# Conditioning scale and shift applied in one step ahead of the first projections, in an adaLN transformer block on one Trainium2 core

## The chip, the core and the metric

The kernel runs on one core of a Trainium2 chip. The metric is device time in microseconds (us) for one execution. Its engines are PE (TensorE, matrix products), DVE (VectorE), ACT (ScalarE), POOL (GpSimd) and SP (SyncE, which here only issues DMAs). Each engine works through its own list in order; semaphores tie the lists together.

## The reference, cut to what matters

```python
# x: (1, 2048, 512) bf16; 32 heads of 16; every query sees 8 keys, 2 rows apart, backwards
mod = (silu(c) @ w_mod).reshape(1, 6, 1, 512)
sa, ca, ga, sb, cb, gb = mod[:, 0..5]            # shift, scale, gate; twice
h = layernorm(x) * (1 + ca) + sa
x = x + ga * A(h, wqkv, wo)      # A: q, k, v = h @ wqkv; softmax over 8 keys; @ wo
h = layernorm(x) * (1 + cb) + sb
x = x + gb * B(h, w1, w3, w2)    # B: (silu(h @ w1) * (h @ w3)) @ w2, F = 1792
```

## The kernel before, in words

The 2048 rows are 16 tiles T of 128 rows. `_build` records some 1200 operations, each with its engine, the values that it reads and writes, and a function that emits it. No run-time scheduler exists: the constant `ORDER` fixes one sequence of all operations, which is split into the five engines' lists, and `SLOTS` gives each temporary value its buffer (8 PSUM banks, and pools of SBUF tiles). `Program.synchronize` then adds only the waits that are needed. Each engine is strictly in order, so one instruction that waits holds up all that stands behind it on that engine. All DMAs but the one for `c` are issued by SP, in order too.

The stages, which overlap:

- **Conditioning.** `c` goes through a tanh (L468), two small POOL operations (L470, L471), a PE transpose (L473) and an ACT copy to `csz` (L475). `scales` (L481) multiplies the scale columns of `w_mod`, by 128-row pieces (512 columns, 1 KB rows, L490), and leaves 1 + ca in `modc`. `warm` (L543) puts in matmuls of ones, whose results are not used. `shifts` (L503) comes later: it forms sa from its own load of 512 KB, and `kb`, the product of sa and wk (32 one-column matmuls, L509).
- **First norm.** `ln_stats` does mean and variance of a tile on DVE (L598, L599), the inverse root on POOL (L603, L605), and the normalised tile `xn` on DVE (L610); tile 3's sums are on ACT (`moments`, L581, L584).
- **First four tiles.** `first_keys` (L700) turns `xn` on PE (L716), scales it without the shift into `h` (L726, L727), multiplies it with wk at 256 columns for tiles 0 and 1 (L735), then for tiles 2 and 3 (L745), adds `kb` on the way out of PSUM (L755), and adds sa to `h` afterwards on DVE (L763) for q and v.
- **Projections.** The other tiles go in groups of four: PE turns (L672), ACT scale and shift (L680), 16 q and 16 k matmuls of 512 columns (L781), and 4 v matmuls a tile (L800). v goes to DRAM and comes back shifted (`values`).
- **Attention.** For each tile DVE makes the products q·k for 8 offsets (L832), PE sums them over each head (L843), DVE and ACT do the softmax for two tiles at a time (L858 to L891), PE turns the weights (L901), DVE multiplies them into the shifted v (L928), PE sums (L936). The sums are turned on PE and copied by ACT for tiles in `EARLY` (0 to 3; L949, L953), whose shifted v comes in 4 KB packets; for the others an SP DMA turns them, and v comes in 2 KB packets. Then wo (L962) and the residual (L966).
- **Feed-forward.** Second norm, w1 and w3 matmuls (L978), silu and product, w2 (L1021, L1009), residual (L1037), store. These are interleaved with the attention of later tiles.

Of the kernel before, what the change touches and what calls it, by code (L numbers as in the profile page):

```python
# [7 lines left out]
ALU = mybir.AluOpType  # L8
AX = mybir.AxisListType

P = 128
# [257 lines left out]
EARLY = frozenset((0, 1, 2, 3))  # L269
PACKET = {T: 170 if T in EARLY else 88 for T in range(16)}  # L270
WMOD = 66
WKP = 88
WARMS = (8, 1, 1, 1, 3)
NVB = 6
NOB = 4
DMA_T = (3, 2)
KEV = (0, 1, 2, 3)
STACT = (3,)
UPACT = frozenset((g, f) for g in range(4) for f in range(14))
GBLATE = False  # L280
LN1 = [[0, 1, 2, 3], [4, 5, 6, 7], [8, 9, 10, 11], [12, 13, 14, 15]]


def _build(p, A_x, A_wqkv, A_wo, B_w1, B_w3, B_w2, c, w_mod, out):
# [46 lines left out]
    sab = sb([P, KT], bf, "sab")  # L331
    kb = sb([P, KT], f32, "kb")
# [93 lines left out]
    for T in range(4):  # L426
        p.dma(x_sb[:, T, :], x_view[:, T, :], ("load", 1), (128, 1024), w=[vx[T]])
    vwm0 = [Val(f"wms0_{t}") for t in range(KT)]
    for t in range(KT):
        p.dma(wm_s[0][:, t, D:2 * D], wm_view[:, t, D:2 * D], ("load", 2), (128, 1024), w=[vwm0[t]], again=WMOD)  # L430
    vwq = [Val("wq"), [Val("wk0"), Val("wk1")], Val("wv")]
    vwq[1] = [vwq[1][t % 2] for t in range(KT)]
    wqkv_view = A_wqkv.rearrange("(t p) n -> p t n", p=P)
    for i in range(2):
        p.dma(wqkv[:, i::2, D:2 * D], wqkv_view[:, i::2, D:2 * D], ("load", 4), (256, 1024), w=[vwq[1][i]], again=WKP)
    vwsa = Val("wms0_sa")
    p.dma(wm_s[0][:, :, 0:D], wm_view[:, :, 0:D], ("load", 28), (512, 1024), w=[vwsa])
    for i in (0, 2):
        p.dma(wqkv[:, :, i * D:(i + 1) * D], wqkv_view[:, :, i * D:(i + 1) * D], ("load", 3 + i), (512, 1024), w=[vwq[i]])
    for g in range(1, 4):  # L440
        p.dma(x_sb[:, 4 * g:4 * g + 4, :], x_view[:, 4 * g:4 * g + 4, :], ("load", 5 + g), (512, 1024), w=vx[4 * g:4 * g + 4])
# [20 lines left out]
    for g in range(NG):  # L462
# [7 lines left out]
    p.op("pool", lambda e: e.tensor_scalar(thc[:], thc[:], 1.0, None, op0=ALU.add), 250, k, w=[vthc])  # L470
    p.op("pool", lambda e: e.tensor_tensor(c4s[:], thc[:], c4[:], ALU.mult), 300, k, r=[vthc, vcT], w=[vc4])  # L471
# [3 lines left out]
    p.op("act", lambda e: e.activation(csz[:, :, 7], bank(vpc).bitcast(bf)[:, 0:KT], ACT.Copy, scale=0.5), 180, ("mod", 1),  # L475
         r=[vpc, vcsz], w=[vcs])

    vca, vsa, vsab, vkb, vmodB = Val("ca"), Val("sa"), Val("sab"), Val("kb"), Val("modB")
    vg = [Val("ga"), Val("gb")]

    def scales():  # L481
        k = ("mod", 2)
        vm = Val("ps_mod", psum)

        def mm(e, t):
            b = bank(vm)
            if t == 0:
                e.matmul(b[:, 0:KT], ident[:], mbase[:, 4:8], start=True, stop=False)
            for j in range(KT):
                ins = e.matmul(b[:, 0:KT], wm_s[0][:, t, D + j * P:D + (j + 1) * P], csz[:, t, 7 - j:11 - j], start=False,  # L490
                               stop=(t == KT - 1 and j == KT - 1))
            return ins

        o = None
        for t in range(KT):
            after = warm(WARMS[t])
            o = p.op("pe", lambda e, t=t: mm(e, t), (4 + (t == 0)) * 27, k, r=[vwm0[t], vcs, vident, vbase] + wm_hold, part=[vm],
                     after=after + ([o] if o else []))
            last[0] = o
        p.op("dve", lambda e: e.tensor_copy(modc[:, 4:8], bank(vm)[:, 0:KT]), 100, k, r=[vm], w=[vca])  # L500

    def shifts():
        k = ("mod", 11)  # L503
        vm, vb = Val("ps_mod", psum), Val("ps_kb", psum)

        def columns(e, v, lhs, rhs):
            for j in range(KT):
                for t in range(KT):
                    ins = e.matmul(bank(v)[:, j:j + 1], lhs[:, t, j * P:(j + 1) * P], rhs(t), start=(t == 0), stop=(t == KT - 1))  # L509
            return ins  # L510

        p.op("pe", lambda e: columns(e, vm, wm_s[0], lambda t: csz[:, t, 7:8]), 16 * 27, k, r=[vwsa, vcs] + wm_hold, w=[vm])
        p.op("dve", lambda e: e.tensor_copy(sab[:], bank(vm)[:, 0:KT]), 100, k, r=[vm], w=[vsab])
        p.op("dve", lambda e: e.tensor_copy(modc[:, 0:4], bank(vm)[:, 0:KT]), 100, k, r=[vm], w=[vsa])
        p.op("pe", lambda e: columns(e, vb, wqkv[:, :, D:2 * D], lambda t: sab[:, t:t + 1]), 16 * 27, ("mod", 12),
             r=[vsab] + vwq[1] + qkv_hold, w=[vb])
        p.op("dve", lambda e: e.tensor_copy(kb[:], bank(vb)[:, 0:KT]), 100, ("mod", 12), r=[vb], w=[vkb])

    def modulation():
        k = ("mod", 3)  # L520
        vm = Val("ps_mod", psum)

        def mm(e):
            b = bank(vm)
            e.matmul(b[:, 0:8], ident[:], mbase[:], start=True, stop=False)
            for t in range(KT):
                for j in range(8):
                    ins = e.matmul(b[:, 0:8], wm_s[1][:, t, j * P:(j + 1) * P], csz[:, t, 7 - j:15 - j], start=False,
                                   stop=(t == KT - 1 and j == 7))
            return ins  # L530

        p.op("pe", mm, 33 * 27, k, r=[vwms[1], vcs, vident, vbase] + wm_hold, w=[vm])
        p.op("dve", lambda e: e.tensor_copy(modc[:, 8:16], bank(vm)[:, 0:8]), 100, k, r=[vm], w=[vmodB])
# [43 lines left out]
    def moments(T):  # L577

        k = ("st", T)
        vs, vb, vm, vv, vn = Val("sum"), Val("nmean"), Val("mean"), Val("var"), Val("xn", xnpool)  # L580
        p.op("act", lambda e: e.activation(vn.at[:], x_sb[:, T, :], ACT.Identity, accum_out=sx[:, T, :]), c_act(512) + 212, k,  # L581
             r=[vx[T]], w=[vs, vn])
        p.op("dve", lambda e: e.tensor_scalar(nm[:, T, :], sx[:, T, :], -D ** -1.5, None, op0=ALU.mult), C_TINY, k, r=[vs], w=[vb])
        p.op("act", lambda e: e.activation(vn.at[:], x_sb[:, T, :], ACT.Square, bias=nm[:, T, :], scale=D ** -0.5,  # L584
                                           accum_out=mv[:, T, 1:2]), c_act(512) + 212, k, r=[vx[T], vb], w=[vv, vn])
        p.op("dve", lambda e: e.tensor_scalar(mv[:, T, 0:1], sx[:, T, :], 1.0 / D, None, op0=ALU.mult), C_TINY, k, r=[vs], w=[vm])
        return [vv, vm]

    def ln_stats(Ts):
# [3 lines left out]
        for T in Ts:  # L593
            vs, vm = Val("st"), Val("mv")
            if T in STACT:
                vms += moments(T)
                continue
# [5 lines left out]
        o = p.op("pool" if i > 1 else "dve", lambda e: e.tensor_scalar(rsn, mv[:, i:i + n, 1], EPS, None, op0=ALU.add), 250 if i > 1 else C_TINY, k,  # L603
                 r=vms, w=[va])
        p.op("pool", lambda e: e.tensor_tensor(rsn, rsn, bass.AP(cst, 0, [[1, P], [0, n]]), ALU.pow), 600, k, r=[va, vcst],  # L605
             w=[vr], lead=o if i > 1 else None)
# [36 lines left out]
    def ln_T(which, gi, vns):  # L643
        vh = Val("h", hpool)
        vh.pieces = None
        k0 = 2 * (gi + 1) if not which else 2 * gi + 2 * len(LN1) + 2
        modv = [vmodB] if which else [vca, vsa]
        n = len(vns)
        if gi >= DMA_T[which]:
            k = ("tr", k0)  # L650
# [530 lines left out]
```

## Time and profile before

| what | value |
|---|---|
| median of the runs | 242.81 us (242.54 to 243.16, 3 runs) |
| the profiled execution: its own time | 241.96 us |
| its span in the profile | 239.9 us |
| PE busy | 232.0 us (97%) |
| DVE busy | 169.0 us (70%) |
| ACT busy | 159.9 us (67%) |
| POOL busy | 20.6 us (9%) |
| DMA moved | 39.92 MB, mean 166 GB/s |

The profile is of one execution. About 2.1 us of its own time lie outside its span. A busy time counts an instruction from start to end; PE's matmuls overlap, so for PE the distance from one start to the next (the pitch) is used where work is added up.

### The profile page before, as it was taken

How to read it: one execution, taken by the hardware profiler on the slowest of the kernel's cores; microseconds unless marked ns; L12 is line 12 of the kernel's file. 1: busy time of each engine (PE TensorE's matmuls, PEld its weight loads, DVE VectorE, ACT ScalarE, POOL GpSimd, SP SyncE). 2: the span in 40 equal slices, each digit the busy share in tenths (PEclk: the TensorE clock that was granted, in tenths of full speed). 3: DMA queues.
4: the chain of work that ended last, by engine and by line, in shares of the span. 5: the costliest groups of instructions: out<-in, count | busy, mean ns of one | idle time of the engine just before them, and what ended most of it. 6: DMA issues, size and time to landing. Idle time of an engine off the chain costs nothing.

```text
span 239.9 us, 4608 instructions
## 1 busy us (share of the span) xinstructions
PE 232.0 (97%) x1803; PEld 135.6 (57%) x1831; DVE 169.0 (70%) x295; ACT 159.9 (67%) x328; POOL 20.6 (9%) x53
## 2 busy tenths in 40 slices
PE   7899999999999999999999999999999999999995
PEld 2655546444578766764444444444654446686774
DVE  5588999999999999989999687282531412334342
ACT  4349786799999987698768898775745385231310
POOL 5524020002001000110000110010000010000000
PEclk9999999999999999999999999999999999999999
DMA  6999788599899698799751864613310001200011
GB/s 172 286 359 300 229 268 256 110 344 378 281 305 321 216 247 212 209 286 192 210 147 36 261 223 117 174 67 68 104 49 0 4 0 44 68 0 22 3 45 44
DMA packets 43418, 39.92 MB, mean 166 GB/s; under 512 B 17249, under 2 KB 35717, under 8 KB 43397
## 3 DMA queue, kind: packets, MB, share of 16 engines
q1 hardware_dynamic: 43389, 39.63, 56.5%
q8 instruction: 14, 0.23, 0.4%
q14 instruction: 7, 0.06, 0.1%
q10 hardware_dynamic: 8, 0.00, 0.0%
HBM read 29.62 MB, written 6.33 MB: 150 GB/s over the span
## 4 chain that ended last, share of the span: by engine, by line
PE 87%; DMA 4%; SPq 3%; DVE 2%; ACT 1%; issue 1%
PE pall L978 41%; PE pall L1021 18%; PE pall L781 8%; PE pall L962 5%; DMA sb_x<-in_A_x_dram 4%; PE pall L800 4%; PE pall L936 3%; PE pall L843 3%; SPq L124 3%; PE pall L1009 3%; DVE sb_st L598 1%; PE pall L672 1%; PE pall L901 1%; DVE sb_xn L610 0%; ACT sb_hh L988 0%
## 5 line engine op out<-in xcount | busy, mean ns | idle before, releaser
L978 PE MATMUL pall<-sb_h,sb_w 128*128 128x256 bf16 (+1 forms) x666 | 102.4, 308 | 0.4 <-issue 0.2
L978 PEld LDWEIGHTS pall<-sb_h,sb_w 128*128 128x128 bf16 x672 | 64.9, 98 | 36.2 <-ACT sb_sg L984 0.9
L984 ACT ACTIVATE sb_sg<-pall 128x256 bf16<-128x256 f32 (+1 forms) x84 | 35.6, 458 | 27.5 <-PE pall L978 27.1
L1021 PE MATMUL pall<-sb_w,sb_hh 128*128 128x512 bf16 x189 | 44.6, 379 | 0.5 <-issue 0.2
L988 ACT ACTIVATE sb_hh<-pall 128x256 bf16<-128x256 f32 (+1 forms) x56 | 26.5, 499 | 17.6 <-PE pall L978 17.3
L832 DVE TENSOR_TENSOR sb_pq<-sb_q,sb_kT 128x4096 bf16<-128x4096 bf16 x16 | 36.1, 2279 | 0.0
L928 DVE TENSOR_TENSOR sb_vsh<-sb_vsh,sb_al 128x4096 bf16<-128x4096 bf16 x14 | 31.9, 2286 | 0.2 <-ACT sb_al L905 0.2
L1021 PEld LDWEIGHTS pall<-sb_w,sb_hh 128*128 128x128 bf16 x196 | 19.0, 98 | 20.9 <-issue 0.4
L781 PE MATMUL pall<-sb_h,sb_wqkv 128*128 128x512 bf16 x106 | 26.0, 379 | 0.4 <-issue 0.2
L989 DVE TENSOR_TENSOR sb_hh<-sb_sg,sb_hh 128x256 bf16<-128x256 bf16 (+1 forms) x56 | 17.8, 352 | 9.0 <-ACT sb_hh L988 8.9
L1037 DVE TENSOR_TENSOR sb_o<-pall,sb_x 128x512 bf16<-128x512 f32 (+1 forms) x18 | 11.2, 628 | 16.6 <-PE pall L1021 12.9
L992 DVE TENSOR_TENSOR sb_hh<-sb_sg,pall 128x256 bf16<-128x256 bf16 x28 | 10.8, 418 | 15.8 <-PE pall L978 11.6
L966 DVE SCALAR_TENSOR_TENSOR sb_x<-pall,sb_x 128x512 bf16<-128x512 f32 x16 | 10.8, 686 | 11.5 <-PE pall L962 11.5
L781 PEld LDWEIGHTS pall<-sb_h,sb_wqkv 128*128 128x128 bf16 x112 | 10.2, 98 | 11.9 <-issue 1.1
L630 POOL TENSOR_SCALAR sb_rs<-sb_var 128x2 f32<-128x2 f32 x8 | 2.5, 314 | 155.5 <-ACT sb_xn L624 155.5
L962 PE MATMUL pall<-sb_wo,sb_ot 128*128 128x512 bf16 x61 | 15.4, 379 | 0.3 <-issue 0.2
L800 PE MATMUL pall<-sb_wqkv,sb_h 128*128 128x512 bf16 x58 | 14.8, 379 | 0.4 <-issue 0.2
L657 ACT ACTIVATE sb_h<-sb_h,sb_modc 128x512 bf16<-128x512 bf16 (+1 forms) x20 | 13.5, 727 | 0.9 <-DMA sb_h<-sb_xn 0.9
L635 ACT ACTIVATE sb_xn<-sb_x,sb_nb,sb_rs 128x512 bf16<-128x512 bf16 x16 | 12.5, 818 | 1.9 <-DVE sb_nb L632 1.9
L942 ACT ACTIVATE sb_oa<-pall 128x512 bf16<-128x512 f32 x16 | 9.3, 604 | 4.7 <-PE pall L936 4.7
L624 ACT ACTIVATE sb_xn<-sb_x,sb_nm 128x512 bf16<-128x512 bf16 x16 | 11.6, 725 | 1.1 <-DVE sb_nm L620 1.0
L789 ACT ACTIVATE sb_q<-pall 128x512 bf16<-128x512 f32 x16 | 9.5, 607 | 3.6 <-PE pall L781 3.6
(114 smaller groups left out, 235.8 us busy)
## 6 DMA issues: line engine op xcount, KB each, us to landing
sb_vsh<-v_scratch_dram SPq DMA_DIRECT2D x40, 256.0 KB, 3.5
v_scratch_dram<-sb_v SPq DMA_DIRECT2D x16, 256.0 KB, 4.7
sb_vsh<-v_scratch_dram SPq DMA_DIRECT2D x8, 512.0 KB, 6.4
sb_w<-in_B_w_dram SPq DMA_DIRECT2D x6, 512.0 KB, 8.9
sb_w<-in_B_w_dram SPq DMA_DIRECT2D x6, 384.0 KB, 6.5
sb_vshx<-v_scratch_dram SPq DMA_DIRECT2D x8, 256.0 KB, 4.1
out_dram<-sb_o SPq DMA_DIRECT2D x14, 128.0 KB, 1.8
sb_x<-in_A_x_dram SPq DMA_DIRECT2D x3, 512.0 KB, 10.1
```

Source lines behind the costliest of these rows:

```text
L635: p.op("act", lambda e, vn=vn, T=T: e.activation(vn.at[:], x_sb[:, T, :], ACT.Identity, bias=nb[:, T, :], scale=rs[:, NT + T, :]), c_act(5 ...
L657: return e.activation(vh.at[:, ft, 0:n * P], vh.at[:, ft, 0:n * P], ACT.Identity, bias=modc[:, 8 * which + ft:8 * which + ft + 1], scale=m ...
L781: ins = e.matmul(bank(vp)[:, 0:n], wqkv[:, t, kind * D + ft * P:kind * D + (ft + 1) * P], vh.at[:, t, 0:n], start=(t == ORDER[0]), stop=(t ...
L800: ins = e.matmul(bank(vp), vh.at[:, t, tt * P:(tt + 1) * P], wqkv[:, t, 2 * D:3 * D], start=(t == ORDER[0]), stop=(t == ORDER[-1]))
L832: return e.tensor_tensor(vp.at[:], in0, in1, ALU.mult)
L928: return e.tensor_tensor(v_w, v_w, a_w, ALU.mult)
L962: ins = e.matmul(bank(vy), vt.at[:, ft, :], wo[:, ft, :], start=(ft == 0), stop=(ft == KT - 1))
L978: ins = e.matmul(bank(vp)[:, 0:n], wt[:, t, fi * P:(fi + 1) * P], vh.at[:, t, 0:n], start=(t == 0), stop=(t == KT - 1))
L984: p.op("act", lambda e: e.activation(vt.at[:, 0:n], bank(vgp)[:, 0:n], ACT.Silu), c_act(n), k, r=[vgp], w=[vt], table="silu")
L988: p.op("act", lambda e: e.activation(vh_.at[:, 0:n], bank(vup)[:, 0:n], ACT.Copy), c_act(n), k, r=[vup], w=[vh_])
L989: p.op("dve", lambda e: e.tensor_tensor(vh_.at[:, 0:n], vt.at[:, 0:n], vh_.at[:, 0:n], ALU.mult), 60 + n * 69 // 128, k, r=[vt], w=[vh_], ...
L1021: ins = e.matmul(bank(vz), vhh[fi].at[:, tt * P:(tt + 1) * P], w2[:, fi, :], start=(fi == 0), stop=(fi == NF - 1))
```

## The change

Scale and shift of the first norm are formed together, before anything is projected. `scales` and `shifts` go; `modulation(0)` multiplies both halves (8 columns at once) from rows of 2 KB, in four loads of 256 KB, as `modulation(1)` does for the second norm. `first_keys`, `moments`, `kb` and the late addition of sa go. Tiles 0 and 1, and tiles 2 and 3, become two groups of `ln_T`, whose ACT and DVE evictions apply scale and shift; q and k are both multiplied at 256 columns for these groups, and for the first group each matmul waits only for its own piece of `h` and its half of wk or wq. The loads come in a new order (tiles 0 and 1, w_mod, wk in halves, tiles 2 and 3, wq in halves, wv, and so on). Tiles 2 and 3 leave `EARLY`, so their sums are turned by DMA, and their shifted v comes in 2 KB packets. The small conditioning steps move from POOL and ACT to DVE, `ln_stats` adds epsilon on POOL for tiles 0 and 1 too, `warm` is called 21 times and not 14, and `ORDER` and `SLOTS` are new throughout.

```diff
-EARLY = frozenset((0, 1, 2, 3))
+EARLY = frozenset((0, 1))
-WARMS = (8, 1, 1, 1, 3)
+WARMS = (8, 3, 2, 2, 6)
+DEV = 2
-DMA_T = (3, 2)
-KEV = (0, 1, 2, 3)
-STACT = (3,)
+DMA_T = (4, 2)
-LN1 = [[0, 1, 2, 3], [4, 5, 6, 7], [8, 9, 10, 11], [12, 13, 14, 15]]
+LN1 = [[0, 1], [2, 3], [4, 5, 6, 7], [8, 9, 10, 11], [12, 13, 14, 15]]
...
-    for T in range(4):
+    for T in range(2):
         p.dma(x_sb[:, T, :], x_view[:, T, :], ("load", 1), (128, 1024), w=[vx[T]])
     for t in range(KT):
-        p.dma(wm_s[0][:, t, D:2 * D], wm_view[:, t, D:2 * D], ("load", 2), (128, 1024), w=[vwm0[t]], again=WMOD)
+        p.dma(wm_s[0][:, t, :], wm_view[:, t, 0:1024], ("load", 2), (128, 2048), w=[vwm0[t]], again=WMOD)
+    p.dma(x_sb[:, 2:4, :], x_view[:, 2:4, :], ("load", 27), (256, 1024), w=vx[2:4])
...
-    p.dma(wm_s[0][:, :, 0:D], wm_view[:, :, 0:D], ("load", 28), (512, 1024), w=[vwsa])
+    for i in range(2):
+        p.dma(wqkv[:, i::2, 0:D], wqkv_view[:, i::2, 0:D], ("load", 3), (256, 1024), w=[vwq[0][i]])
+    p.dma(wqkv[:, :, 2 * D:3 * D], wqkv_view[:, :, 2 * D:3 * D], ("load", 5), (512, 1024), w=[vwq[2][0]])
+    for T in (4, 6):
+        p.dma(x_sb[:, T:T + 2, :], x_view[:, T:T + 2, :], ("load", 6), (256, 1024), w=vx[T:T + 2])
...
-    p.op("pool", lambda e: e.tensor_scalar(thc[:], thc[:], 1.0, None, op0=ALU.add), 250, k, w=[vthc])
-    p.op("pool", lambda e: e.tensor_tensor(c4s[:], thc[:], c4[:], ALU.mult), 300, k, r=[vthc, vcT], w=[vc4])
+    p.op("dve", lambda e: e.scalar_tensor_tensor(c4s[:], thc[:], 1.0, c4[:], op0=ALU.add, op1=ALU.mult), 180, k,
+         r=[vthc, vcT], w=[vc4])
+    p.op("dve", lambda e: e.tensor_scalar(c4s[:], c4s[:], 0.5, None, op0=ALU.mult), 180, k, w=[vc4])
...
+        for ts in ([(t,) for t in range(KT)] if i == 0 else [tuple(range(KT))]):
+            after = warm(WARMS[ts[0]]) if i == 0 else []
+            o = p.op("pe", lambda e, ts=ts: mm(e, ts), (8 * len(ts) + (ts[0] == 0)) * 27, k,
+                     r=[vwms[1]] * i + [vwm0[t] for t in ts] * (1 - i) + [vcs, vident, vbase] + wm_hold, part=[vm],
+                     after=after + ([o] if o else []))
+        p.op("dve", lambda e: e.tensor_copy(modc[:, jlo:jlo + 8], bank(vm)[:, 0:8]), 100, k, r=[vm], w=[vmod[i]])
...
+        vh.pieces = [Val(f"h_{ft}") for ft in range(KT)] if not which and not gi else None
...
+                def ev_dve(e, j=j, vt=vt, half=half):
+                    ft = 2 * half + j
+                    b = bank(vt).bitcast(bf)
+                    return e.tensor_scalar(vh.at[:, ft, 0:n * P], b[:, j * 512:j * 512 + n * P],
+                                           modc[:, 8 * which + 4 + ft:8 * which + 5 + ft],
+                                           modc[:, 8 * which + ft:8 * which + ft + 1], op0=ALU.mult, op1=ALU.add)
...
-            o = p.op("pe", lambda e, t=t: mm(e, (t,)), c_mm(n), k, r=[vh.pieces[t]] + vw + qkv_hold, part=[vp], hold=[vh],
+            o = p.op("pe", lambda e, t=t: mm(e, (t,)), c_mm(n), k, r=[vh.pieces[t], vw[t]] + qkv_hold, part=[vp], hold=[vh],
...
-    scales()
+    modulation(0)
     warm(WARMS[4])
-    shifts()
     for gi, Ts in enumerate(LN1):
-        if gi == 0:
-            vh = first_keys([[v for T in (0, 1) for v in ln_stats([T])], ln_stats([2, 3])])
-        else:
-            vh = ln_T(0, gi, [v for pr in pairs(Ts) for v in ln_stats(pr)])
+        vns = [v for pr in ([[T] for T in Ts] if gi == 0 else pairs(Ts)) for v in ln_stats(pr)]
+        vh = ln_T(0, gi, vns)
         proj_qk(gi, Ts, 0, vh)
-        if gi:
-            proj_qk(gi, Ts, 1, vh)
+        proj_qk(gi, Ts, 1, vh)
```

## The prediction

> **What bounds the kernel now.** First the page: PE's share, then where in the span it is idle.
>
> ```profile
> span 239.9 us, 4608 instructions
> PE 232.0 (97%) x1803; PEld 135.6 (57%) x1831; DVE 169.0 (70%) x295; ACT 159.9 (67%) x328; POOL 20.6 (9%) x53
> ...
> PE   7899999999999999999999999999999999999995
> PEld 2655546444578766764444444444654446686774
> DVE  5588999999999999989999687282531412334342
> ```
>
> PE is full from the third slice to the last but one. DVE is full with it up to slice 21 (126 us). The windows, with each engine's busy time:
>
> ```profile
> 0.00:8.40 8.40, 6.39 (x40) 2.51 (x40) 5.27 (x18) 4.16 (x9) 4.77 (x20) 1.00 0.68 203
> 8.40:14.00 5.60, 4.84 (x70) 4.16 (x72) 2.59 (x12) 0.92 (x3) 2.00 (x6) 1.00 0.99 317
> ...
> 40.00:60.00 20.00, 19.73 (x179) 9.76 (x180) 19.74 (x21) 18.49 (x36) 1.35 (x2) 1.00 0.85 269
> 60.00:80.00 20.00, 19.84 (x197) 14.38 (x199) 19.62 (x26) 19.79 (x49) 1.02 (x2) 1.00 0.93 304
> ```
>
> Columns: stretch, length, then PE, PEld, DVE, ACT, POOL; granted clock, DMA share, GB/s. So any order that lets DVE start its attention work later must either have DVE catch up or make PE wait. The timeline gives the few real PE gaps, DVE's first product and a late meeting of both:
>
> ```profile
> 8.46 1.03 PE L735 MATMUL pall<-sb_h,sb_wqkv 128*128 128x256 bf16 x8 [0.45 <-DVE sb_xn L610]
> 11.43 0.54 PE L509 MATMUL pall<-sb_csz,sb_wm_s 128*128 128x1 bf16 x16 [0.62 <-DMA sb_wm_s<-in_w_mod_dram]
> 22.47 0.29 PE L672 MATMUL pall<-sb_ident,sb_xn 128*128 128x128 bf16 x2 [0.44 <-DVE sb_xn L610]
> 24.77 4.46 DVE L832 TENSOR_TENSOR sb_pq<-sb_q,sb_kT 128x4096 bf16<-128x4096 bf16 x2
> 112.66 2.28 DVE L928 TENSOR_TENSOR sb_vsh<-sb_vsh,sb_al 128x4096 bf16<-128x4096 bf16 x1
> 115.07 1.04 PE L936 MATMUL pall<-sb_vsh,sb_ind 128*32 128x512 bf16 x16
> ```
>
> By distances between matmul starts the gaps are 0.6 us before 8.46, 0.8 before 11.43 and 0.6 before 22.47; after that none above 0.3 us but for matmuls missing from the records. The first gap really ends with wk's first half, which landed at 8.33. Nothing behind 22.5 us can be won by better order; the change can win only in the front or by less PE work, and any wait that it adds costs in full.
>
> **PE work.** Pitches from the trace: 0.216 us for 512 columns, 0.109 for 256, 0.058 for a 128-column turn, 0.026 for a 1- to 8-column matmul. Gone: 32 shift matmuls (0.83), 8 turns of tiles 2 and 3 (0.46). Scale and shift together are 33 small matmuls for 17 (+0.42); q of the first four tiles is 32 x 0.109 for 16 x 0.216 (+0.03). Sum about -0.9. The seven added warm-up matmuls lie ahead of the first projection, where PE waits for loads anyway.
>
> **Loads of the front.** The trace's landing records give, for the queue of before: 0.5 MiB at 4.67 us, 1.0 at 6.63, 1.25 at 8.33, 1.5 at 9.54, 2.0 at 11.30, 2.5 at 12.85, 3.0 at 14.34, 3.5 at 15.85, 4.0 at 18.70. In the new queue the end of w_mod stands at 1.25 MiB, wk's halves at 1.5 and 1.75, tiles 2 and 3 at 2.0, wq's halves at 2.25 and 2.5, wv at 3.0, tiles 4/5 at 3.25, 6/7 at 3.5, 8 to 11 at 4.0. Longer rows bring nothing by themselves: in the packet records 1 KB took 51 ns and 2 KB (the later w_mod load, the shifted v) 101 to 103. Bigger loads do help: SP needs 0.46 us to issue each, and at 128 KB each the DMA engines were idle for 14% of 2.2 to 6.7 and 6% of 6.7 to 9.6, together 0.8 us.
>
> ```profile
> 2.20:6.70 4.50, 4.39 (x28) 1.59 (x27) 3.49 (x12) 2.48 (x7) 2.26 (x5) 1.00 0.86 245
> 6.70:9.60 2.90, 2.45 (x28) 1.71 (x25) 1.99 (x6) 0.84 (x2) 2.46 (x7) 1.00 0.94 305
> ...
> 12.90:16.00 3.10, 3.02 (x31) 1.76 (x31) 2.43 (x10) 0.79 (x2) 0.04 (x1) 1.00 1.10 367
> ```
>
> Landings are thus the old ones at equal bytes, less 0 to 0.8; I take 0.4, as part of that idle will be landing skew.
>
> **The new front, walked.** w_mod ends at 7.9. Eight matmuls (0.2), the copy to `modc` (0.16), two evictions each on DVE (0.3 each) and ACT (0.4 each), and six warm-ups: first k matmul at about 9.4, 0.9 later than now. PE then follows the loads: wk's halves, wq's first (11.7), wq's second (12.45), and 11 matmuls after it: 13.65. Tiles 2 and 3 land at 10.9; two statistics (0.64 each), aggregates (0.2), POOL's pair (0.26 + 0.71), two normalisations (0.4 each) and hand-overs put their turns at 14.3 to 14.8. Tile 3's statistics now cost DVE 0.7, but the four additions of sa (1.2) are gone. From 14.8 PE has v, 24 q/k matmuls and v again (5.2 us): 20.0. Then turns, both gates, 8 q/k and 4 v matmuls (4.4 us), with a stall on the normalised tile 7: DVE has evictions until 15.6, four statistics to 18.2, two normalisations to 19.2, the statistics of 8 and 9 (landed 18.3) to 20.5, tile 7 at 21.3, where PE would be at 20.9: 0.5. So the projections of tiles 4 to 7 begin at 24.9 (24.5 to 25.4). Lateness (start of a row less the pitches ahead of it, so all idleness and half-speed so far) is 24.9 - 19.4 = 5.5 there, against 5.9 before at 29.27. All pitches sum to 230.4 (with the warm-ups, +1.5) against 229.9. By PE alone: 5.5 + 230.4 - 5.9 - 229.9 = +0.1 us. ACT does not decide: its 256-column evictions follow at 0.27 us, its 512-column ones at 0.48, and it loses two turned-sum copies (0.74 each) and tile 3's sums (1.7 us).
>
> **DVE behind it.** Before the first product DVE still has statistics of 10 to 13, four normalisations, four aggregates and the two gate copies. The same from 20.05 to 24.77 before took 4.7 us with one statistic more and a copy less: 4.4. First product at 25.7 (25.3 to 26.2), against 24.77. From there to the end of tile 9's weighting DVE has the same list in both kernels: 14 products, 10 weightings, 28 feed-forward products, 8 residuals, five softmax ends, the wo scaling and four of w2. It took 114.86 - 24.77 = 90.1 us, so tile 9 is ready at 115.9. PE's sum of it began at about 115.55 (half of the row above is tile 8's), with 120.6 us of pitches behind; now 121.1 lie behind, as the new order keeps more for later. So +0.35 + 0.5 = +0.85 us. This is the later path, and the forecast: span 239.9 + 0.9 = 240.8, that execution 242.8; on the median 242.81 + 0.9 = 243.7. Since DVE sat idle about 1.9 us within those 90 us, the term can fall to the +0.1 above (below, if the loads are early); with 26.2 and another 0.5 us of waits it is +1.9.
>
> **Tiles 2 and 3 by DMA.** SP gets two more turns (1.25 us each to issue, landing in 2.4 to 5.1) and four more loads of v. PE's turn and ACT's copy go; PE has 4 us of other rows before it needs the result, so I cost them at nothing. Without that cover each is 2 to 4 us late. Behind the two turns SP holds a v store and the loads of v for tiles 4 and 5; they wait for ACT's copies at about 66, would issue from 68.5, and land by 74.4 and 77.5, against use from 77.3 and 80. The margin is about 3 us.
>
> **Small moves.** POOL's two conditioning steps (0.53 and 0.42) become two on DVE and the copy to `csz` moves from ACT to DVE (0.15 to 0.2 each, by L603 and L475). They push tile 1's statistics back by about 0.6, and epsilon for tiles 0 and 1 goes from DVE (0.15) to POOL (0.2 to 0.4 each). Both normalised tiles are then ready by about 7.0, under w_mod's end at 7.9; were w_mod landed at 6.5, they would cost 0.5. On SP the zero rows go ahead of tiles 12 to 15; v's first store, which waited for them until 25.5 before, comes about 4 us earlier and hides behind DVE's products, as it did. The second w_mod half (1 MiB) goes behind three v stores; it landed at 25.9 and is used near 41, so a delay of 5 us stays hidden. The new PE waits for wq's halves hold up all of PE's list, the turns of tiles 2 and 3 first; they are in the walk.
>
> **Rivals.** (A) *The loads run at full rate and the front wins.* With the 367 GB/s of 12.9 to 16.0 held from 2.2 on, w_mod ends at 6.5, tiles 2/3 at 8.6, wv at 11.5, the normalised tile 7 at 19.0, PE's projections of 4 to 7 at 22.6 and the first product at 23.4, 2.3 earlier than in the walk: 0.85 - 2.3 = -1.4, so 241.4. Against it: 245 and 305 GB/s in the first two stretches, although 86 and 94% busy. The Trainium skill, DMA: Bandwidth & Descriptors, "Where 436 GB/s comes from", gives about 358 GB/s as the limit of a core's HBM side; by that rule the time would be about A's. The trace reaches it only after 12.9. 14%.
> (B) *DVE catches up*, using its idle 1.9 us, and PE's +0.1 is all: 242.9. For it: later idle DVE stretches exist. Against: 99% busy from 24 to 100. 22%.
> (C) Forecast, DVE late by 0.9: 243.7. 46%.
> (D) *SP's queue decides.* The v loads of tiles 4 and 5 stand behind the two new turns, with DMA at 0.93 in 60 to 80, and weight loads between. It decides if they land over 3 us later than walked; at 4.5, DVE waits 1.5 us on top of C: 245.2. 18%. That w_mod's rows do not go faster is already in the sum.
>
> **Numbers.** About 0.3%, 0.73 us, is what can be told from no change: 242.08 to 243.54. Slower: C less a tenth of it, and D: 0.60. Same: B and that tenth, 0.25. Faster: A and a bit of B, 0.15. The range takes in the ends of C and B and most of D: 242.2 to 245.4; the far half of A and a tail of D stay out.
>
> **What would show it.** Right: first k matmul near 9.4, a PE wait before wq's halves, first L832 product at 25.3 to 26.2, PE gaps ending with DVE's L928 between 90 and 116. Wrong: that product before 24.8 (A); late, but no PE gap later (B); DVE gaps that end with a load of `sb_vsh` for tiles 4 and 5 near 77 us (D); PE gaps ended by ACT, which no case has.

## The result, and the profile after

The changed kernel takes 241.31 us (median of 17 runs, 239.84 to 242.82), the kernel before 242.78 in the same sessions (17 runs): ratio 0.9943, 95% interval 0.9921 to 0.9965, so 1.4 us (0.9 to 1.9) faster. The forecast was 243.7, slower by 0.9; what came is rival A's time. The profiled execution took 241.22 us, against 241.96 before.

The page of the changed kernel, the same rows:

```profile
span 239.2 us, 4643 instructions
...
PE 233.7 (98%) x1830; PEld 137.7 (58%) x1830; DVE 169.4 (71%) x289; ACT 158.0 (66%) x329; POOL 19.1 (8%) x53
...
PE   7999999999998999999999999999999999999995
PEld 2677545545676875664444444444556447586874
DVE  4589999999999999899998977437215222242442
```

PE is full from the second slice; the 8 in slice 13 (72 to 78 us) is new. The windows (columns as before: stretch, length, PE, PEld, DVE, ACT, POOL, clock, DMA share, GB/s):

```profile
0.00:8.40 8.40, 6.89 (x58) 3.29 (x59) 3.62 (x10) 1.59 (x2) 4.08 (x20) 1.00 0.72 236
8.40:14.00 5.60, 5.60 (x52) 4.25 (x49) 3.64 (x12) 2.83 (x8) 1.95 (x5) 1.00 1.09 357
2.20:6.70 4.50, 4.50 (x29) 1.79 (x28) 2.49 (x8) 0.76 (x2) 1.53 (x4) 1.00 0.94 301
6.70:9.60 2.90, 2.90 (x38) 1.75 (x35) 1.68 (x5) 0.87 (x2) 2.53 (x9) 1.00 1.05 358
9.60:12.90 3.30, 3.30 (x31) 2.89 (x30) 2.15 (x8) 0.92 (x3) 0.94 (x2) 1.00 1.10 358
12.90:16.00 3.10, 3.10 (x27) 2.02 (x26) 2.46 (x8) 2.66 (x7) 0.10 (x1) 1.00 1.10 348
40.00:60.00 20.00, 20.00 (x176) 10.03 (x173) 20.00 (x22) 18.17 (x35) 0.93 (x2) 1.00 0.84 271
60.00:80.00 20.00, 18.84 (x188) 14.04 (x187) 18.95 (x30) 18.61 (x46) 0.93 (x2) 1.00 0.82 240
```

The kernel before had, from 9.6 to 12.9 us:

```profile
9.60:12.90 3.30, 2.68 (x41) 2.26 (x38) 1.47 (x8) 0.84 (x2) 1.01 (x3) 1.00 0.98 308
```

Two things are to be seen. The DMA engines moved 301, 358 and 358 GB/s in the three stretches from 2.2 to 12.9 us, where they had moved 245, 305 and 308; and PE, which was idle for 0.8 of the 5.6 us from 8.4, is never idle there. Between 60 and 80 us PE has lost 1.2 us instead of 0.2. The timeline, PE and DVE:

```profile
9.64 3.66 PE L675 MATMUL pall<-sb_h,sb_wqkv 128*128 128x256 bf16 x32
13.13 0.61 PE L623 MATMUL pall<-sb_ident,sb_xn 128*128 128x128 bf16 x8
24.04 4.48 DVE L726 TENSOR_TENSOR sb_pq<-sb_q,sb_kT 128x4096 bf16<-128x4096 bf16 x2
77.19 1.05 PE L872 MATMUL pall<-sb_h,sb_w 128*128 128x256 bf16 x8 [1.16 <-DMA sb_w<-in_B_w_dram]
112.64 2.28 DVE L822 TENSOR_TENSOR sb_vshx<-sb_vshx,sb_al 128x4096 bf16<-128x4096 bf16 x1
115.19 0.60 PE L830 MATMUL pall<-sb_vshx,sb_ind 128*32 128x512 bf16 x8
```

The first projection starts at 9.64 (forecast 9.4), and all 32 follow without a gap, where the walk had PE wait for wq's second half. The turns of tiles 2 and 3 are at 13.13 (14.3 to 14.8), the first product at 24.04 (25.7). Landings, from the same records as before: w_mod 7.43 us (8.33 before at equal bytes), wk 8.15 and 8.86, tiles 2/3 9.61 (11.30), wq 10.35 and 11.10 (12.85 for the second), wv 12.61 (14.34), tiles 6/7 14.11 (15.85). They are 0.9 to 1.7 us earlier, where the prediction took 0.4. Landings move between executions: in the seven profiles with the same front (runs 7 to 11 and 16 are the others) w_mod ended at 7.2 to 8.0 us, tiles 2/3 landed at 9.6 to 10.2, wq's second half at 11.1 to 11.7, and the first product started at 23.87 to 24.35.

The wait at 77 us is seen on SP's queue (start, length, queue):

```profile
53.81 3.49 SPq L124 DMA_DIRECT2D sb_w<-in_B_w_dram  x4
63.39 3.74 SPq L124 DMA_TRANSPOSE sb_ot<-sb_oa  x2
67.18 0.58 SPq L124 DMA_DIRECT2D v_scratch_dram<-sb_v  x1
67.81 3.11 SPq L124 DMA_DIRECT2D sb_vsh<-v_scratch_dram  x5
70.97 0.59 SPq L124 DMA_DIRECT2D sb_w<-in_B_w_dram  x1
```

SP has nothing to issue from 57.3 to 63.39: it waits for ACT's copies for the two new turns. The load at 70.97, w3's third piece, stands behind them and landed at 77.15.

### The profile page after: what moved, and what is told of

The parts are those of the page before. It is cut to its first block, busy times and chain, and to the rows that moved or that the text cites. A ratio compares the mean times of both kernels' runs of the same rounds, so it can differ in the third digit from the quotient of the medians.

```text
span 239.2 us, 4643 instructions
## 1 busy us (share of the span) xinstructions
PE 233.7 (98%) x1830; PEld 137.7 (58%) x1830; DVE 169.4 (71%) x289; ACT 158.0 (66%) x329; POOL 19.1 (8%) x53
## 4 chain that ended last, share of the span: by engine, by line
PE 90%; DMA 4%; ACT 2%; SPq 1%; issue 0%; DVE 0%; ACTq 0%
PE pall L872 37%; PE pall L915 16%; PE pall L675 12%; PE pall L694 5%; PE pall L856 4%; PE pall L737 3%; PE pall L511 3%; PE pall L830 3%; DMA sb_w<-in_B_w_dram 3%; PE pall L903 3%; DMA sb_ot<-sb_oa 2%; PE pall L623 2%; SPq L124 1%; ACT sb_hh L882 1%; PE pall L489 1%; PE pall L795 1%
## 5 line engine op out<-in xcount | busy, mean ns | idle before, releaser
L675 PE MATMUL pall<-sb_h,sb_wqkv 128*128 128x512 bf16 (+1 forms) x160 | 30.4, 336 | 0.0
L822 DVE TENSOR_TENSOR sb_vsh<-sb_vsh,sb_al 128x4096 bf16<-128x4096 bf16 x12 | 27.3, 2286 | 3.2 <-DMA sb_vsh<-v_scratch_dram 1.7
L886 DVE TENSOR_TENSOR sb_hh<-sb_sg,pall 128x256 bf16<-128x256 bf16 x28 | 10.9, 418 | 18.5 <-PE pall L872 13.7
L675 PEld LDWEIGHTS pall<-sb_h,sb_wqkv 128*128 128x128 bf16 x160 | 15.1, 98 | 11.4 <-issue 0.4
L631 ACT ACTIVATE sb_h<-pall,sb_modc 128x256 bf16<-128x256 bf16 (+1 forms) x20 | 12.0, 654 | 6.7 <-DVE sb_modc L500 5.8
L694 PE MATMUL pall<-sb_wqkv,sb_h 128*128 128x512 bf16 x64 | 16.3, 379 | 0.0
L856 PE MATMUL pall<-sb_wo,sb_ot 128*128 128x512 bf16 x64 | 15.8, 380 | 0.3 <-ACT sb_oa L836 0.3
L583 POOL TENSOR_SCALAR sb_rs<-sb_var 128x2 f32<-128x2 f32 x8 | 1.8, 226 | 152.0 <-ACT sb_xn L577 152.0
L683 ACT ACTIVATE sb_q<-pall 128x512 bf16<-128x512 f32 (+1 forms) x20 | 10.1, 519 | 3.0 <-PE pall L675 3.0
```

What stands on the lines that cost most here:

```text
L675: ins = e.matmul(bank(vp)[:, 0:n], wqkv[:, t, kind * D + ft * P:kind * D + (ft + 1) * P], vh.at[:, t, 0:n], start=(t == ORDER[0]), stop=(t ...
L694: ins = e.matmul(bank(vp), vh.at[:, t, tt * P:(tt + 1) * P], wqkv[:, t, 2 * D:3 * D], start=(t == ORDER[0]), stop=(t == ORDER[-1]))
L822: return e.tensor_tensor(v_w, v_w, a_w, ALU.mult)
L856: ins = e.matmul(bank(vy), vt.at[:, ft, :], wo[:, ft, :], start=(ft == 0), stop=(ft == KT - 1))
```

## Experiments

The theories: **theory 1**, the gain comes from the front's loads, since eight issues of 128 KB had left the DMA engines short of work; rival **2**, the 2 KB rows themselves; **3**, less PE work; **4**, the new order. Theories and rivals with higher numbers are stated in the expectations that use them. Ratios are to the kernel before, with 95% intervals; the changed kernel's is 0.9943 [0.9921, 0.9965], and 0.001 is 0.24 us.

**1. Bigger front loads alone, in the old kernel.**

```diff
-    for T in range(4):
+    for T in range(2):
         p.dma(x_sb[:, T, :], ...
+    p.dma(x_sb[:, 2:4, :], x_view[:, 2:4, :], ("load", 1), (256, 1024), w=vx[2:4])
-    for t in range(KT):
-        p.dma(wm_s[0][:, t, D:2 * D], ...
+    for t in (0, 2):
+        p.dma(wm_s[0][:, t:t + 2, D:2 * D], ...
```

> The kernel before with only the sizes of three front loads changed: tiles 2 and 3 come by one load of 256 KB instead of two of 128 KB, and the four 128 KB pieces of w_mod's scale by two loads of 256 KB. Nothing else moves: same matmuls, same order. Theory 1 (SyncE needs about 0.46 us to issue a load, so eight loads of 128 KB feed the DMA engines at only some 280 GB/s, they run dry between 4.5 and 6.5 us, and every later load lands late): the first half of wk, which landed at 8.33 us, lands at 7.3 to 7.7; the loads behind it land 0.9 to 1.5 us earlier than before; the TensorE gaps at 7.6, 10.5 and 21.7 us (2.0 us in all) shrink by half or more, and the time falls by 0.7 to 1.4 us (ratio 0.994 to 0.997). Rival 3 (the gain of the change is TensorE work taken away, scale and shift in one pass): this kernel has all the old work, so the time stays within 0.3 us of before. Rival 4 (the new order brings the gain): the same, no change.

0.9984 [0.9952, 1.0017]. The landings did what theory 1 says; windows:

```profile
6.70:9.60 2.90, 2.90 (x25) 1.78 (x24) 1.48 (x6) 1.14 (x4) 1.96 (x7) 1.00 1.07 365
9.60:12.90 3.30, 3.30 (x43) 2.58 (x42) 1.73 (x5) 0.94 (x3) 1.45 (x4) 1.00 1.09 353
```

365 and 353 GB/s in place of 305 and 308, and 1.5 MiB landed at 8.56 us instead of 9.54, 2.0 at 10.14 instead of 11.30. But in the paired loads w_mod's first piece came with the second, PE waited 0.9 us for it, its matmuls then ran at half speed to 10.6 us (last section), and the first product came at 25.38. That execution took 243.70 us, 1.7 above the run's median, so the others need not have started as slowly. So the issue size sets the landings, as theory 1 has it; the time does not tell the theories apart.

**2. Smaller front loads in the changed kernel.** Its w_mod loads become eight of 128 KB, tiles 2 and 3 two.

```diff
-        p.dma(wm_s[0][:, t, :], wm_view[:, t, 0:1024], ...
+        p.dma([wm_s[0][:, t, a:a + D] for a in (D, 0)], [wm_view[:, t, a:a + D] for a in (D, 0)], ...
-    p.dma(x_sb[:, 2:4, :], x_view[:, 2:4, :], ...
+    p.dma([x_sb[:, T, :] for T in (2, 3)], [x_view[:, T, :] for T in (2, 3)], ...
```

> The changed kernel with w_mod's four loads of 256 KB in 2 KB rows issued as eight of 128 KB in 1 KB rows (scale half, then shift half of each piece) and tiles 2 and 3 by two loads of 128 KB; all else, order and matmuls, as in the changed kernel. Theory 1: SyncE issues twelve small loads, 5.5 us, ahead of wk instead of six; the first half of wk lands 0.8 to 1.3 us later than the 8.15 us of the changed kernel and all behind it too; the time rises by 0.7 to 1.3 us over the changed kernel, to about that of the kernel before (ratio to before 0.998 to 1.000). Rivals 3 and 4 (less TensorE work, the new order): the time stays that of the changed kernel, ratio 0.994.

0.9976 [0.9948, 1.0003]: 0.8 us of the 1.4 are given back, the intervals overlap. In the profile w_mod ended at 8.68, wk's first half landed at 9.48, tiles 2 and 3 landed at 11.29, the first product started at 26.20, all later than in any of the seven profiles with the larger loads. On theory 1's side, not alone decisive.

**3. Rows of 1 KB in the same four loads.**

```diff
-    wm_s = [at([P, KT, 1024], ...
+    wm_s = [at([P, 2, KT, D] if i == 0 else [P, KT, 1024], ...
-        p.dma(wm_s[0][:, t, :], wm_view[:, t, 0:1024], ...
+        p.dma(wm_s[0][:, :, t, :], wm_view[:, t, 0:1024].rearrange("p (a d) -> p a d", a=2), ...
```

> The changed kernel with w_mod's first 1024 columns laid out in SBUF as two halves, so that each of the four 256 KB loads writes rows of 1 KB instead of 2 KB; the issues, their bytes and their order are the same. Theory 1 (bytes for each issue decide): landings within 0.2 us of the changed kernel, time within 0.3 us of it (ratio to before 0.993 to 0.996). Rival 2 (the 2 KB rows themselves are what is faster): w_mod ends 0.5 to 1 us later than 7.43 us, the time is 0.5 to 1 us above the changed kernel (ratio 0.996 to 0.999).

0.9944 [0.9914, 0.9974], the changed kernel's own ratio: by the time, rival 2 falls. Its one profile does not agree: w_mod ended at 7.96 us and tiles 2 and 3 landed at 10.57, 0.5 and 1.0 later than in the changed kernel's first profile, as rival 2 expected, and the latter is outside the 9.6 to 10.2 of the seven. That execution, 243.18 us, is the slowest of the run's twelve, and with 2 KB rows w_mod too has ended as late as 8.01. So the row length is shown to be worth no time within 0.7 us; what it does to the landings stays open.

**4. wk issued by ACT's queue in the old kernel.**

```diff
-        p.dma(wqkv[:, i::2, D:2 * D], ..., again=WKP)
+        p.dma(wqkv[:, i::2, D:2 * D], ..., again=WKP, eng="act")     # in ORDER behind the tanh
```

> The kernel before with one thing changed: the two loads of wk (256 KB each) are issued by ScalarE's queue, behind its first instruction (tanh) at about 3 us, instead of as ninth and tenth load of SyncE at 4.55 us. Sizes, rows, matmuls and order stay. Theory 1 (SyncE's issue rate left the DMA engines idle between 4.5 and 6.5 us): the DMA engines stay busy there, wk's halves land before 8.3 and 9.5 us (7.3 to 8.0 and 8.0 to 8.8), w_mod's shift half lands at 10.0 to 10.7 us instead of 11.30, the TensorE gap at 11.4 us (0.6 us) goes, and the time falls by 0.3 to 1.0 us (ratio 0.996 to 0.999). Rivals 3 and 4 (the gain is less TensorE work or the new order): ratio 1.000 within 0.0015. Against theory 1 would also be landings as before.

1.0054 [1.0025, 1.0083], slower, against every theory's number. wk and the shift half did land early (wk at 6.43 and 7.54 for 8.33 and 9.54, 2.0 MiB at 10.09), but they came ahead of w_mod's pieces, which SP was still issuing and which landed at 7.11 to 8.59 instead of 5.03 to 6.63:

```profile
PE pall L488 <- DMA sb_wm_s<-in_w_mod_dram: 1.9, 1, 1.9
```

PE waited 1.9 us for w_mod's first piece, and the first product came at 26.54. Early loads are worth something only behind those that the chain needs first.

**5 and 6. The landings put back where the walk had them.** Tiles 12 to 15 (512 KB), then tiles 8 to 11 too, go ahead of wk in the changed kernel's order. Nothing else moves.

```diff
 # ORDER, loads only (33 is tiles 8 to 11, 34 is tiles 12 to 15)
-    21, 22, 23, 24, 26, 27, 25, 28, 29, ..., 30, 31, 32, 33, ..., 34
+    21, 22, 23, 24, 34, 26, 27, 25, 28, 29, ..., 30, 31, 32, 33, ...          # one load
+    21, 22, 23, 24, 32, 34, 26, 27, 25, 28, 29, ..., 30, 31, 33, ...          # two loads
```

> The changed kernel with one load moved: tiles 12 to 15 (512 KB) stand ahead of wk's first half instead of behind the zero rows, so that wk, tiles 2 and 3, wq, wv and tiles 4 to 7 land about 1.46 us later (512 KB at 358 GB/s), which is about where the prediction's walk put them (wk 9.6 and 10.3, tiles 2/3 11.1, wq 11.8 and 12.6, wv 14.1, tiles 6/7 15.6 us); the end of w_mod, all matmuls and all other places stay. Theory 11 (the mis-sized landings are the whole error of the prediction): the first product starts at 25.2 to 26.0 us and the time is 1.0 to 1.7 us above the changed kernel (ratio to before 0.998 to 1.002). Rival 12 (the loads behind w_mod have slack, the walk put the first product late for another reason): the first product stays at 24.0 to 24.6 us and the ratio at 0.993 to 0.996.

1.0016 [0.9982, 1.0050]: 1.8 us (0.8 to 2.7) above the changed kernel, no better than the old one.

> The same with tiles 8 to 11 moved there as well, 1 MiB in all ahead of wk, so that wk and all behind it up to tiles 6/7 land about 2.9 us later than in the changed kernel. Theory 11: first product at 26.6 to 27.5 us, the time 2.4 to 3.2 us above the changed kernel (ratio 1.004 to 1.007); against the run with half of it, a slope near one. Rival 12: less than 1.5 us.

1.0081 [1.0048, 1.0113]: 3.3 us (2.4 to 4.3) above. For 1.46 and 2.93 us of delay, worked out from the bytes, the time rises by 1.8 and 3.3, a slope near one. PE's wait and the first product in the run with one load:

```profile
11.07 1.83 PE L675 MATMUL pall<-sb_h,sb_wqkv 128*128 128x256 bf16 x14 [0.74 <-DMA sb_wqkv<-in_A_wqkv_dram]
26.61 4.49 DVE L726 TENSOR_TENSOR sb_pq<-sb_q,sb_kT 128x4096 bf16<-128x4096 bf16 x2
```

(In that execution w_mod itself ended at 8.38, 1.0 late, and tiles 2 and 3 landed at 12.44, 2.8 later than in the changed kernel's profile; so its product is later than the 25.2 to 26.0 that was expected. The execution was 1.5 us longer than the changed kernel's for a product that was 2.6 later. With two loads the product came at 27.03.) The loads behind w_mod have no slack to speak of: rival 12 falls, and the time is as theory 11 has it. That the landings are the whole error, which theory 11 also says, is taken up in the next section.

**7 and 8. Which engine sets the end: 2 us more on each.** The product that run 7 doubles, tile 0's, is the second in DVE's order, not the first (tile 1's comes first), so DVE's work is later from about 29 us on; run 8's matmuls ran from 48.2 to 50.3.

```diff
+            if T == 0:                                # run 7: tile 0's product twice
+                p.op("dve", prod, C_PQ, ("pq", T), r=[vq[cch]] + ks, w=[vp], lock=True)
             prods[T] = p.op("dve", prod, ...
...
         def wop(e):                                   # run 8: ten more matmuls
+            for _ in range(10 if T == 0 else 0):
+                e.matmul(bank(vy), ones[:, 0:P], ones[:], start=True, stop=True)
```

> The changed kernel with VectorE's first product (tile 0, 2.24 us) computed twice, so that all VectorE work from 24 us on comes 2.24 us later. Step of the prediction (the time of the first product goes to the end one for one): the time rises by 1.9 to 2.4 us over the changed kernel (ratio to before 1.002 to 1.004). Rival 8 (TensorE's own work sets the end in the changed kernel and VectorE has slack of a microsecond or more): it rises by 0 to 1.2 us (ratio 0.994 to 0.999).

1.0019 [0.9994, 1.0044]: 2.24 us on DVE cost 1.8 (1.0 to 2.7).

> The changed kernel with ten more matmuls of 128x512 (213 ns each, 2.1 us) on TensorE ahead of tile 0's output projection, at about 52 us. Rival 8 (TensorE's own work sets the end): the time rises by 1.7 to 2.3 us over the changed kernel (ratio to before 1.001 to 1.004). Step of the prediction (VectorE's chain sets the end, TensorE's work waits for it): it rises by 0 to 1 us (ratio 0.994 to 0.998).

1.0017 [0.9996, 1.0039]: 2.1 us on PE cost 1.8 (1.1 to 2.5), where the prediction's step expected 0 to 1. So what is late before 50 us on either engine is paid at 80 to 86%, with intervals that reach down to a half. Which engine sets the end the two runs do not tell, since each delay reached the other engine. In run 7 PE waited 1.4 us at 31.1 for the doubled product (total, times, longest):

```profile
PE pall L734 <- DVE sb_pq L726: 1.4, 1, 1.4
```

In run 8 DVE waited 2.0 us, up to 51.4, for tile 0's output projection, which stands behind the added matmuls. The changed kernel's profile has neither wait.

**9 and 10. The wait at 77 us.** w3's third piece (48) goes right behind the other weight loads (47), ahead of the turns; the same kernel was run twice.

```diff
-    ..., 47, ..., 422, ..., 432, ..., 48, ...
+    ..., 47, 48, ..., 422, ..., 432, ...
```

> The changed kernel with one load moved in SyncE's order: the third piece of w3 is issued right behind the other weight loads at about 57 us, ahead of the two new transposing DMAs of tiles 2 and 3, instead of behind them at 71 us. Theory 5 (a part of the front's gain is given back at 76 us, where TensorE waits 1.3 us for this load because the transposing DMAs hold the queue): that gap disappears and the time falls by 0.9 to 1.4 us below the changed kernel (ratio to before 0.988 to 0.991). Rival 6 (VectorE's shares of the attention set the end there, TensorE's gap is only taken up elsewhere): the gap goes but TensorE waits as long at the next sums or products; the time falls by less than 0.4 us (ratio 0.993 to 0.996).

> The third piece of w3 early in SyncE's order, as in the earlier run (ratio 0.991), once more. Two runs with this move and others in it gave 0.995 and 0.996, with new TensorE waits of 0.9 to 1.9 us behind it. If the move itself is worth the 1.3 us of the wait that it removes: ratio 0.989 to 0.992. If that wait is taken up by another behind it (rival 6): 0.993 to 0.996, and TensorE waits again between 85 and 100 us.

0.9913 [0.9883, 0.9943] and 0.9931 [0.9903, 0.9960]: 0.7 and 0.3 us under the changed kernel, neither resolved from it. The wait was gone in both; others came behind it. The first run, DVE then PE, and the second run's list of waits (total, times, longest):

```profile
93.18 2.29 DVE L822 TENSOR_TENSOR sb_vsh<-sb_vsh,sb_al 128x4096 bf16<-128x4096 bf16 x1 [2.21 <-DMA sb_vsh<-v_scratch_dram]
95.53 0.61 PE L830 MATMUL pall<-sb_vsh,sb_ind 128*32 128x512 bf16 x8 [1.93 <-DVE sb_vsh L822]
```

```profile
PE pall L856 <- ACT sb_oa L836: 1.2, 1, 1.2
```

So new PE waits of 1.9 and 1.2 us stand behind the one of 1.2 that was removed; what is left of the gain is too small to be told.

**11. The v loads of tile 7 early as well.**

```diff
-    ..., 489, ..., 464, ..., 490, ..., 491, ..., 492, ...        # 464: tile 5's turn
+    ..., 489, 490, 491, 492, ..., 464, ...
```

> The changed kernel with two moves in SyncE's order: the third piece of w3 ahead of the transposing DMAs of tiles 2 and 3 (as in the run before this one), and the last three of tile 7's four v loads ahead of tile 5's transposing DMA instead of behind it. In that earlier run the wait of 1.3 us at 76 us was gone, but TensorE waited 1.9 us at 93.6 us for tile 7's weighting, whose v loads were issued between 83.6 and 87.8 us and landed at 93.2. Theory 5 (places in SyncE's queue decide both waits): tile 7's loads are issued by 86.2 us and land before 91 us, that wait goes too, and the time falls by 1.0 to 2.5 us below the changed kernel (ratio to before 0.984 to 0.990). Rival 7 (the loads are late because the DMA engines are slow there, whenever they are issued): the wait at 93 us stays, ratio 0.990 to 0.993.

0.9957 [0.9937, 0.9977], a miss. The wait for tile 7's loads was gone, but tile 5's turn, now behind them, kept PE 1.7 us at L856. SP's queue there has no free place: what is moved up moves something else back.

**12. A quicker start.** Run 9's move; tile 1's x issued by ACT; tile 1's statistics ahead of the copy to `csz`; two warm-ups cut short.

```diff
-        p.dma(x_sb[:, T, :], x_view[:, T, :], ("load", 1), (128, 1024), w=[vx[T]])
+        p.dma(x_sb[:, T, :], ..., w=[vx[T]], eng="act" if T else "sp")
-                return e.matmul(bank(vw), ones[:, 0:P], ones[:], start=True, stop=True)
+                n = 512 if i < 19 else 16
+                return e.matmul(bank(vw)[:, 0:n], ones[:, 0:P], ones[:, 0:n], start=True, stop=True)
 # ORDER: 48 behind 47, 20 (tile 1's x) behind 18 (c), 91 and 92 (tile 1's statistics) behind 87 (tile 0's)
```

> The changed kernel with four moves: the third piece of w3 early in SyncE's order (the earlier run with this alone gave a ratio of 0.991); tile 1's x issued by ScalarE's queue, so that SyncE issues w_mod one place sooner; tile 1's bn_stats and bn_aggr ahead of the copy of the silu columns on VectorE, which waits for TensorE; and the last two of the 21 warm-up matmuls cut from 512 columns to 16, since TensorE is still at them when the first piece of h is ready. Theory 5 and 9 (what comes sooner at the front comes off the end nearly one for one): w_mod ends 0.3 to 0.5 us sooner, tile 1's turns too, the first k matmul starts at 8.7 to 9.2 us instead of 9.64, the first product at 23.2 to 23.8 instead of 24.04, and the ratio to before is 0.986 to 0.990. Rival 8 (TensorE's own work sets the end, the front's start is only filled with warm-ups and waits): 0.990 to 0.994.

0.9951 [0.9920, 0.9981], a miss. In its profile w_mod's third piece landed at 6.15 us (6.44 in the changed kernel's first profile), but of the last piece the first of its 16 parts came at 6.47 and the last at 8.76, so the first projection started at 9.94 and the first product at 25.20.

**13. The two warm-ups alone.**

```diff
-                return e.matmul(bank(vw), ones[:, 0:P], ones[:], start=True, stop=True)
+                n = 512 if i < 19 else 16
+                return e.matmul(bank(vw)[:, 0:n], ones[:, 0:P], ones[:, 0:n], start=True, stop=True)
```

> The changed kernel with only the last two of the 21 warm-up matmuls cut from 512 columns to 16. In the changed kernel the last of them ends at 9.63 us and the first k matmul starts at 9.64, while the first piece of h was written by 9.1 to 9.2. If those warm-ups hold the front, the first k matmul and the first product start 0.3 to 0.45 us sooner, and the time falls by as much (ratio to before 0.992 to 0.9935). If h or wk holds it, nothing moves (ratio 0.994), and TensorE waits where the warm-ups were.

0.9959 [0.9927, 0.9990]: no gain shown. Its profile caught a slow start (last section), so whether the warm-ups hold the front stays open.

**14 to 16. Unchanged kernels profiled again.**

> The kernel before once more, unchanged, for a second profiled execution. Theory 9 (the profiled execution of before that the prediction worked from, 241.96 us against a median of 242.8, had a quicker front than most: landings move by some tenths of a microsecond from one execution to the next, and the first product and with it the end move along): the first product of tile 0 starts at 25.0 to 26.0 us instead of 24.77, w_mod's scale half ends later than 6.63 us, and the execution's own time less the start of the first product is again 217.0 to 218.0 us (241.96 - 24.77 = 217.2). Rival 10 (executions differ somewhere behind the front): the first product starts within 0.2 us of 24.77.

> The kernel before a third time, unchanged, with the same expectations as for the second: first product at 25.0 to 26.0 us by theory 9, 24.6 to 25.0 by rival 10, own time less that start 217.0 to 218.0 us by theory 9.

Own times 242.44 and 241.59, first products at 24.36 and 24.09: theory 9 falls, and rival 10's 24.6 to 25.0 was missed as well. The profile that the prediction worked from had the latest first product of the three. Own time less that start was 218.1 and 217.5 (217.2 in the first). Its landings were repeated too: 1.25 MiB at 9.09 and 8.84 (8.33), 2.0 MiB at 11.34 and 11.07 (11.30).

> The changed kernel once more, unchanged, for a second profiled execution: the first product within 0.4 us of 24.04 us (three runs with the same front gave 23.93 to 24.73), own time less that start 217.0 to 218.5 us, and the wait for the third piece of w3 at 76 us again 1.0 to 1.6 us.

241.91 us, first product at 23.87, as expected; the wait at 76 us was only 0.5, a miss, but PE waited 1.9 us for tile 7's weighting at 95. Both profiles of the changed kernel thus have a wait of one to two us between 75 and 96 us; which it is changed from one to the other.

No version was shown to be faster than the changed kernel. No run isolates rival 3 or 4: PE's work did shrink (next section), and that may be part of the 1.4 us over the old kernel.

## Why the prediction was wrong

- **PE work, -0.9: right.** With every matmul counted at its full-speed pitch, the two repeated profiles of before (no record missing) sum to 224.07 us, the changed kernel to 224.70. Less seven warm-ups of 0.213 (1.49), the rest has shrunk by 0.86 (the prediction's own terms add up to -0.84).
- **Loads of the front, "the old ones at equal bytes, less 0 to 0.8; I take 0.4": this term was mis-sized.** It measured 0.9 at w_mod's end and 1.4 to 1.7 behind it. The prediction had seen the 0.46 us for each issue, but it priced the loss as the time in which the DMA engines were idle up to 9.6 us, 0.8 us. By bytes the loss is twice that: at 245, 305 and 308 GB/s the old kernel had moved 570 KB less by 12.9 us than the changed one at 301, 358 and 358, which is 1.6 us at 358 GB/s; its two repeated profiles, by the same sum, lack 1.7 and 1.2. The busy shares hid it: the prediction took 0.86 and 0.94 against 1.00, where its own row of 12.9 to 16.0 shows 1.10 while 367 GB/s were moved. Run 1 shows that the size of the issues brings this in the old kernel (2.0 MiB at 10.14 for 11.30), and run 2 that small issues take it back in the changed one (tiles 2 and 3 at 11.29 for 9.61); run 3 shows that the rows bring no time. The "landing skew" for which the prediction halved its 0.8, the lag from the first to the last of a load's 16 parts, differs between executions about as much as between the kernels: for the load that ends at 2.0 MiB it was 1.9, 1.3 and 1.7 us in the old kernel and 0.8 to 1.5 in the changed one, and the old kernel's profile with 1.3 landed no earlier (11.34).
- **The walk as far as w_mod: nearly right** (first projection 9.4, measured 9.64). From there it followed landings that were too late by 0.9 to 1.4: wq's second half 12.45 against 11.10, tiles 2/3 10.9 against 9.61. So the projections of tiles 4 to 7 began at 23.98 and not 24.9, the first product at 24.04 (23.87 to 24.35 in seven profiles) and not 25.7.
- **Is that the whole error?** Runs 5 and 6 delay these landings: with 1.46 us the gain is gone (ratio 1.0016, 243.2 us on the prediction's base), with 2.93 it is 0.8% slower. The sign of the forecast hung on this term. With 0.9 to 1.7 instead of 0.4, "by PE alone" gives -0.4 to -1.2 us, and DVE's sum, with the measured 24.04 for 25.7, gives 0.85 - 1.66 = -0.8. The first pair of profiles has -0.74; that this agrees is partly luck, as the other pairs of the three old and two changed ones lie between +0.3 and -1.2. The unprofiled runs say -1.4 (0.9 to 1.9), so some 0.6 us of the gain (0.1 to 1.1) has no term here. The base itself was a late one: the old kernel's three first products average 24.41, the seven of the changed front 24.10, so the lead over the old kernel is 0.3 us and not the 0.73 of the first pair.
- **"Any wait costs in full", and DVE's lateness goes to the end: borne out in the main** for work added before 50 us, by runs 7 and 8, at 80 to 86%; for the wait at 77 us it is not shown, as its removal gave 0.7 and 0.3 us of 1.2 (runs 9 and 10), neither resolved. That DVE's path is the later one, by 0.75 us over "by PE alone", is not borne out: the delay on PE cost as much. The 90.1 us from the first product to the end of the second of two weightings near 113 us were 90.9 (by the order it is tile 8's before and tile 9's after, not tile 9's in both): DVE gave back 0.8 of its lead, 0.6 of it waiting for v loads.
- **Tiles 2 and 3 by DMA, "at nothing": wrong by the later waits.** Rival D named the place, SP's queue behind the two turns, but not the victim: v's loads for tiles 4 and 5 cost DVE 0.6 us in two waits (one repeat of the old kernel has such a wait of 0.7 too), and w3's third piece, which the prediction did not follow past the turns, cost PE 1.2. Runs 9 and 10 show that little of it can be had back.
- **Rival A** had the time (241.4), though its 2.3 us of lead were 1.66 and its PE path had no room for the waits at 76 to 96 us. Its rule from the Trainium skill, DMA: Bandwidth & Descriptors, "Where 436 GB/s comes from", about 358 GB/s, agrees with the trace: 358, 357 and 348 GB/s in the windows of the changed kernel, 365 and 353 in run 1.

Where the time went, against the mean of the two repeated profiles of before: PE's idle and slow time fell by 2.2 us in the first 40 us, rose by 1.9 from 60 to 100, and fell by 0.8 in the other stretches together; the work at full-speed pitch rose by 0.6 (warm-ups +1.5, all else -0.86). That is about -0.5: 0 against the one profile and -0.9 against the other, whose spans were 0.3 and 1.2 us longer than the changed kernel's; 0.3 us lie outside this count. The changed kernel's second profile, 239.9 us, was 0.4 longer than the one and 0.5 shorter than the other. So pairs of profiles show anything from a loss of 0.4 to a gain of 1.2 us; the 1.4 rest on the unprofiled runs alone, and where all of it arises stays open.

## What to carry to other kernels

Where a kernel starts by loading, compare the bytes moved in the first microseconds with what the same queue moves later. A rate like the 245 GB/s here against 367, with loads of 128 KB that take 0.46 us each to issue, pointed at the issuing engine, and then the size of an issue counted. Price the loss by bytes and not by the idle share, and at the loads that stand last in the stretch. Profile the base more than once before a sum is built on one of its times. And when a turn moves to a DMA queue, follow every load behind it, not only those of its own kind.

## What the runs showed of the hardware that was not expected

**TensorE starts at half speed, and when the full speed comes differs between executions.** Warm-up matmuls of 512 columns start 0.427 us apart at first and 0.215 later. In the seven profiles with the changed kernel's front the step came between 4.7 and 6.8 us. In run 13 w_mod's first piece landed at 5.62 us instead of 4.57, TensorE idled 0.43 us from 5.33, and stayed slow until 10.0. An idle spell alone does not do this: in run 12 TensorE idled 0.33 us from 5.33 as well and was at full speed from 5.9. The warm-ups of run 13, and then the same of the changed kernel (start, busy, count):

```profile
5.99 1.44 PE L512 MATMUL pall<-sb_ones 128*128 128x512 bf16 x3
7.49 1.01 PE L512 MATMUL pall<-sb_ones 128*128 128x512 bf16 x2
8.55 1.01 PE L512 MATMUL pall<-sb_ones 128*128 128x512 bf16 x2
```

```profile
5.41 1.19 PE L511 MATMUL pall<-sb_ones 128*128 128x512 bf16 x3
6.64 0.59 PE L511 MATMUL pall<-sb_ones 128*128 128x512 bf16 x2
7.27 0.59 PE L511 MATMUL pall<-sb_ones 128*128 128x512 bf16 x2
```

Being in order ahead of w_mod's last product, the slow warm-ups put the first projection at 11.21, 1.6 us later, though w_mod had landed at 7.70. The granted clock read 1.00 throughout, so that column does not show it. The Trainium skill, TensorE: Matmul & The Clock Gate, "What's actually happening", tells of an activity window of about 3.4 us that runs on its own, so that the step moves from run to run. The spread of 4.7 to 6.8 and a step put off by some 3 to 5 us agree with it; the window itself no run shows, and why run 13 stayed slow and run 12 did not is open.

**One part of a load can land 2 us behind the others.** In run 9 the last of tile 7's v loads, whose first part had landed at 90.0, ended at 93.2; a 16 KB packet of the instruction queue had taken 2.18 us from 89.4. In the changed kernel's first profile such a packet began at 90.8 and took 2.03 us, and that v load had landed by 91.5; in its second the packet took only 1.22 us from 90.4, and the load's parts came from 90.2 to 93.2. So the packet is not shown to be the cause.
